# A fused attention and mixture-of-experts kernel: its last group of tokens in eight plain products in place of seven with sums

## The chip, the cores and the metric

One Trainium2 chip, of which this kernel uses one core. A core has a matrix engine (TensorE, PE in the profile; its weight loads are PEld), a vector engine (VectorE, DVE), a scalar engine (ScalarE, ACT), a general engine (GpSimd, POOL) and a queue engine for transfers (SyncE, SP). Each works through its own instructions in order; they meet at semaphores. Matmul results land in PSUM, which has eight banks of 128 x 512 fp32 numbers; POOL does not read it in this kernel. The metric is the device time of one execution in microseconds (us); lower is better.

## The reference

Linear attention with exponential features on 8 batches x 8 heads x 576 positions gives x of 4608 x 512. A routing table P of 4608 x 8 comes from x by alternate normalising, and eight experts are added up, every token through every expert:

```python
out = np.zeros((N, D), dtype=np.float32)      # N = 4608, D = 512
for e in range(E):                            # E = 8
    h = np.maximum(x @ w1[e], 0.0)            # w1[e]: 512 x 1024
    ye = h @ w2[e]                            # w2[e]: 1024 x 512
    out += P[:, e:e + 1] * ye
```

## The kernel before

**Tiling.** The tokens are in nine groups of 512: groups 0 to 7 are the first 512 positions of each batch, group 8 is what is left of all batches. The attention comes first, with expert 0 between its pieces; then the experts 1 to 7, one after the other. `acc[g]` holds a group's 512 x 512 fp32 result in SBUF (four blocks `ts` of 128 tokens), and each expert adds to it. The last expert (e = 7) takes group 8 first, then the pairs of groups 0-1, 2-3, 4-5, 6-7, and stores each group's result when it is done.

**Two products per expert and group.** The up-projection (`up7`) makes h in bf16, in tiles `hT` of 128 x 2 x 512: `H[j][k]` of a group is half j of the 1024 hidden features, in two tiles. The down-projection (`down7`) makes h @ w2. Both use a scheme of seven products for a 2 x 2 split in place of eight (Strassen's, in Winograd's form): some operands are sums of quarters. In `down7` the halves are i (256 tokens each), j (hidden features, then output columns). The sums of w2's quarters (`T` tiles) are made once per expert; the last expert leaves w2 itself whole. The sums of h, S0 to S3, are made per group by DVE: eight instructions of 128 x 512 (`sub`, whose `f.tensor_tensor` is L1013), into `S` tiles, and for the very last group into `hT` tiles.

**The seven products** of a group are named X1, X2, X3, X4, Y1, Z1, Z2. Each is eight matmuls of 256 columns (`product`, L1130: two blocks of 128 tokens, four steps over 512 hidden features). They use three PSUM banks, x, y and z. Those of one letter add up in one bank: X1 is done and read out, then X2 is added on top and read out, and so on. Where they go, as (token half, column half) of `acc[g]`: X1 and Y1 to (0,0), X2 and Z2 to (0,1), Z1 and X3 to (1,1), X4 to (1,0). X1 multiplies w2 and h themselves, Y1 also; X2, Z1, X3 and Z2 have a sum of h on the left; X2, Z1, X3, X4 a sum of w2 on the right.

**Reading a product out** (`read`) has two ways. Either DVE does it in two instructions of 128 x 256, bank times P plus `acc` (L1306). Or ACT scales the bank into a tile (two instructions, L1316; tile `V`, in the end `U`) and POOL adds it to `acc` (one of 128 x 512, L1320). ACT's scalings carry a common key, "order of V", so that they run in the order in which they were emitted.

**The order of work** is the program's own. `Plan` collects operations in the order in which the code emits them, with an engine, a duration, a latency and what they depend on, and `Plan.schedule` writes out one order for every engine: at each step it takes the operation that can start earliest, and among those the one emitted first. The chip's engines then follow that order, with semaphores for the true dependencies. The plan holds a few dependencies that are there for order alone: X1 lists the keys of S1 and S2, Z1 that of S3, and POOL's adds at the end those of "sums of h".

**The main loop** interleaves by `ORDER` the up-projection of one pair with the down-projections of the pair before, taken from `queue`. When the last pair, groups 6 and 7 of expert 7, is up, nothing is left to interleave with: `d6` and `d7` are the two down-projections left over, and the list `END` says in which order their products are emitted ("a" for group 6, "b" for group 7). `store` issues the results from SP, for these two groups by quarters as soon as both products of a quarter are in: 256 KB each, and the quarter (1,0) of group 6 in two of 128 KB.

Of the kernel before, what the change touches and what calls it, by code (L numbers as in the profile page):

```python
# [228 lines left out]
def kernel(  # L229
# [1009 lines left out]
    def acc_part(g, i, j):  # L1239
        return lambda: acc[g][:, 2 * i:2 * i + 2, 256 * j:256 * j + 256]  # L1240

    def down7(e, g, H, B7, last=False):


        def part(i, j, h):
            return lambda: H[j][h]()[:, :, 256 * i:256 * i + 256]

        def hk(i, j, h=None):
            if h is None:
                return hk(i, j, 0) + hk(i, j, 1)  # L1250
            return [(H[j][h], i)] if g == 8 else [(H[j][h], n) for n in range(2)]

        def a(i, j):
            return lambda k, n: H[j][k // 2]()[:, k % 2, 256 * i + 128 * n:][:, 0:128]

        late = akey(g)
        S = [new("hT" if last else "S") for _ in range(4)]

        def sv(n):
            return S[n]().rearrange("p a b -> p (a b)").rearrange("p (a b) -> p a b", a=4)  # L1260

        def sh(n, h):
            return lambda: sv(n)[:, 2 * h:2 * h + 2, :]

        def s(n):
            return lambda k, i: sv(n)[:, k, 128 * i:128 * i + 128]

        def sk(n):
            return [(S[n], h) for h in range(2)]

        def s2():
            for h in range(2):
                sub(dve, 512, sh(2, h), part(0, 0, h), part(1, 0, h), ALU.subtract,
                    hk(0, 0, h) + hk(1, 0, h) + ["sums of h"], [(S[2], h)])

        if not last:
            s2()
        for h in range(2):
            sub(dve, 512, sh(0, h), part(1, 0, h), part(1, 1, h), ALU.add,
                hk(1, 0, h) + hk(1, 1, h) + ["sums of h"], [(S[0], h)])  # L1280
        for h in range(2):
            sub(dve, 512, sh(1, h), sh(0, h), part(0, 0, h), ALU.subtract,
                [(S[0], h)] + hk(0, 0, h), [(S[1], h)])
        if last:
            s2()
        for h in range(2):
            sub(dve, 512, sh(3, h), part(0, 1, h), sh(1, h), ALU.subtract,
                [(S[1], h)] + hk(0, 1, h), [(S[3], h)] + (["sums of h"] if h else []))

        def prod(bank, lhs, y, r, first, more=()):  # L1290
            f, r2 = B7[y]
            product(bank, lhs, lambda k: f()[:, k, :], 4,
                    r + r2 + (["P"] if e else late) + list(more), first)

        by_dve = ("X2", "Z2", "X4")
        ending = e == E - 1 and g in (6, 7)
        if ending:
            by_dve = by_dve + ("X3", "Y1", "Z1") if g == 6 else by_dve

        def read(bank, i, j, name):  # L1300

            if name not in by_dve:
                return read2(bank, i, j)
            for n in range(2):
                ts = 2 * i + n
                dve(330, lambda n=n, ts=ts: nc.vector.scalar_tensor_tensor(  # L1306
                    out=acc[g][:, ts, 256 * j:256 * j + 256],
                    in0=bank()[:, 256 * n:256 * n + 256], scalar=P[:, 4 * g + ts, e:e + 1],
                    in1=acc[g][:, ts, 256 * j:256 * j + 256], op0=ALU.mult, op1=ALU.add),
                    [bank, "P"], [("acc", g, ts, j)])  # L1310

        def read2(bank, i, j):

            u = new("U" if ending else "V")
            for n in range(2):
                act(390, lambda n=n: nc.scalar.activation(  # L1316
                    out=u()[:, n, :], in_=bank()[:, 256 * n:256 * n + 256], func=ACT.Copy,
                    bias=0.0, scale=P[:, 4 * g + 2 * i + n, e:e + 1]), [bank, "P"],
                    [(u, n), "order of V"])
            pool(670, lambda: nc.gpsimd.tensor_tensor(  # L1320
                out=acc[g][:, 2 * i:2 * i + 2, 256 * j:256 * j + 256],
                in0=acc[g][:, 2 * i:2 * i + 2, 256 * j:256 * j + 256], in1=u(), op=ALU.add),
                [(u, 0), (u, 1)] + ["sums of h"] * ending,
                [("acc", g, 2 * i + n, j) for n in range(2)])

        if e == 1 and g < 9:
            for ts in range(4):
                act(512, lambda ts=ts: nc.scalar.activation(
                    out=acc[g][:, ts, :], in_=acc[g][:, ts, :], func=ACT.Copy, bias=0.0,
                    scale=P[:, 4 * g + ts, 0:1]), ["P", ("acc", g, ts)] + akey(g)  # L1330
                    + ([("acc", g - 2, 0, 0)] if g >= 2 else []),
                    [("acc", g, ts, j) for j in range(2)])
        x, y, z = new("P1"), new("P1"), new("P1")

        def X1():
            prod(x, a(0, 0), "11", hk(0, 0), True, sk(1) + sk(2))
            read(x, 0, 0, "X1")

        def Y1():
            prod(y, a(0, 1), "21", hk(0, 1), True)  # L1340
            read(y, 0, 0, "Y1")

        def Z1():
            prod(z, s(0), "t1", sk(0), True, sk(3))
            read(z, 1, 1, "Z1")

        def X2():
            prod(x, s(1), "t2", sk(1), False)
            read(x, 0, 1, "X2")

        def X3():
            prod(x, s(2), "t3", sk(2), False)
            read(x, 1, 1, "X3")

        def Z2():
            prod(z, s(3), "22", sk(3), False)
            read(z, 0, 1, "Z2")

        def X4():
            prod(x, a(1, 1), "t4", hk(1, 1), False)  # L1360
            read(x, 1, 0, "X4")

        def stores(names):
            if e < E - 1:
                return
            if g not in (6, 7):
                for ts in range(4 if len(names) == len(all_) else 0):
                    store(g, ts)
                return
            for i, j, by in ((0, 0, {"X1", "Y1"}), (0, 1, {"X2", "Z2"}), (1, 1, {"Z1", "X3"}),  # L1370
                             (1, 0, {"X4"})):
                if by <= names and (i, j) not in stored:
                    stored.add((i, j))
                    one = (g, i, j) == (6, 1, 0)
                    for n in range(2 if one else 1):
                        store(g, 2 * i + n, (j,), 1 if one else 2)

        all_ = {"X1": X1, "Y1": Y1, "Z1": Z1, "X2": X2, "X3": X3, "Z2": Z2, "X4": X4}
        emitted, stored = set(), set()

        def step(name):
            all_[name]()
            emitted.add(name)
            stores(emitted)

        return step


    ORDER = "X1 x10 w10 x11 X2 x20 y10 x21 Z1 y11 X3 w11 x30 x31 x40 x41 w20 Y1 w21 X4 Z2".split()
    END = (  # L1390
        "aX1 bY1 aX2 bX1 bX2 bZ1 aZ1 aX3 aY1 aZ2 bX3 bX4 bZ2 aX4").split()
    queue = []

    def pop():
        if not queue:
            return None
        e, g, H, B7 = queue.pop(0)
        return down7(e, g, H, B7, (e, g) == (E - 1, 7))

    for e in range(1, E):  # L1400
        w1, w2 = load_w(e, ["late"] + [("acc", 8, ts, j) for ts in range(4) for j in range(2)
                                       if e > 1])
        if e == 1:
            for p in range(4):
                pair_sums_x(p)
            sums_x(8)
            for p in range(4):
                seen = {}
                for key in xkeys(2 * p):
                    for d in plan.readers.get(key, []):  # L1410
                        seen[id(d)] = d
                grant("X", p, seen.values())
        A7, B7 = sums_w(e, w1, w2)
        for p in (range(5) if e < E - 1 else (4, 0, 1, 2, 3)):
            X = load_x(p)
            gs = (2 * p, 2 * p + 1) if p < 4 else (8,)
            H = [[[new("hT") for _ in range(2)] for _ in range(2)] for _ in gs]
            un = up7(A7, p, X, H, ["up0"])
            for half in range(len(gs)):
                dn = pop()  # L1420
                for n in ORDER:
                    if len(n) == 3:
                        un[n[:2], int(n[2]) + 2 * half]()
                    elif dn is not None:
                        dn(n)
            queue += [(e, g, h, B7) for g, h in zip(gs, H)]
    d6, d7 = pop(), pop()
    for n in END:
        (d6 if n[0] == "a" else d7)(n[1:])
    plan.run(tc)  # L1430


# [28 lines left out]
```

## Time and profile before

| | |
|---|---|
| time, median of 3 runs | 1035.03 us (1034.81 to 1035.73) |
| the profiled execution: its time | 1034.76 us |
| the profiled execution: its span, first to last instruction | 1032.9 us |
| mean granted clock of TensorE | 0.997 |
| bytes moved by transfers | 93.77 MB |
| seven products of groups 6 and 7, from the first matmul to the start of the last | 1010.92 to 1027.64 us |

In the lines of the profile a matmul or other instruction stands as line, engine, operation, what it writes "<-" what it reads, and "xN" for how many of a kind in a row. In the timeline the first two numbers are the start and the length in us, and a bracket at the end gives idle time of the engine ahead of it and who ended it. Matmuls overlap, so that one lasts 0.27 us though the next follows after 0.11. In the names of a product, `w` is a quarter of w2, `T` a sum of its quarters, `hT` a quarter of h (or, for the last group, a sum in a borrowed tile) and `S` a sum of h.

### The profile page before, as it was taken

How to read it: one execution, taken by the hardware profiler on the slowest of the kernel's cores; microseconds unless marked ns; L12 is line 12 of the kernel's file. 1: busy time of each engine (PE TensorE's matmuls, PEld its weight loads, DVE VectorE, ACT ScalarE, POOL GpSimd, SP SyncE). 2: the span in 40 equal slices, each digit the busy share in tenths (PEclk: the TensorE clock that was granted, in tenths of full speed). 3: DMA queues.
4: the chain of work that ended last, by engine and by line, in shares of the span. 5: the costliest groups of instructions: out<-in, count | busy, mean ns of one | idle time of the engine just before them, and what ended most of it. 6: DMA issues, size and time to landing. Idle time of an engine off the chain costs nothing.

```text
span 1032.9 us, 21788 instructions
## 1 busy us (share of the span) xinstructions
PE 1007.7 (98%) x7856; PEld 692.4 (67%) x7974; DVE 874.4 (85%) x1875; ACT 707.5 (68%) x1571; POOL 466.8 (45%) x535
## 2 busy tenths in 40 slices
PE   7899999999999999999999999999999999999997
PEld 5666666644566766676667666676667666776665
DVE  7999998987787888888878888888888888887887
ACT  7999999845688766566666665666666665656662
POOL 5877775400244444434444354435343444344443
PEclk9999999999999999999999999999999999999998
DMA  9998985095311152122511161106111421104323
GB/s 259 179 171 143 183 156 103 2 230 145 75 43 51 52 107 58 42 63 51 114 42 54 40 128 48 41 22 123 48 47 52 99 65 42 62 22 123 133 92 123
DMA packets 124700, 93.77 MB, mean 91 GB/s; under 512 B 47456, under 2 KB 116640, under 8 KB 124592
## 3 DMA queue, kind: packets, MB, share of 16 engines
q1 hardware_dynamic: 90832, 68.44, 24.3%
q0 software_dynamic: 33680, 23.90, 16.2%
q8 instruction: 62, 1.02, 0.4%
q14 instruction: 46, 0.38, 0.1%
q10 hardware_dynamic: 80, 0.03, 0.0%
HBM read 94.98 MB, written 14.16 MB: 106 GB/s over the span
## 4 chain that ended last, share of the span: by engine, by line
PE 90%; DVE 6%; DMA 1%; issue 1%; ACT 1%; SPq 0%; POOL 0%; DVEq 0%; ACTq 0%
PE P L1130 40%; PE P L1164 30%; PE P L484 17%; DVE acc L1306 1%; PE P L683 1%; DMA acc<-in_q_dram 1%; DVE hT L1194 1%; DVE m L476 1%; DVE w L1013 1%; PE P L722 1%; DVE hT L1013 1%; DVE S L1013 0%; SPq L406 0%; PE P L688 0%; DVE xb L703 0%
## 5 line engine op out<-in xcount | busy, mean ns | idle before, releaser
L1320 POOL TENSOR_TENSOR acc<-acc,V 128x512 f32<-128x512 f32 x244 | 313.9, 1298 | 433.4 <-ACT V L1316 430.0
L1190 ACT COPY U<-P 128x512 f32<-128x512 f32 x378 | 216.2, 588 | 133.4 <-PE P L1164 68.9
L1316 ACT ACTIVATE V<-P 128x256 f32<-128x256 f32 x488 | 212.8, 477 | 122.1 <-PE P L1130 118.6
L1194 DVE CUSTOM_DVE_ANT_0 hT<-P,U 128x512 bf16<-128x512 f32 x378 | 252.3, 687 | 36.6 <-ACT U L1190 21.0
L1130 PEld LDWEIGHTS <-S 128*128 128x128 bf16 x1984 | 194.5, 98 | 56.0 <-issue 3.0
L1306 DVE SCALAR_TENSOR_TENSOR acc<-P,acc 128x256 f32<-128x256 f32 x384 | 164.7, 478 | 72.4 <-PE P L1130 69.9
L1164 PE MATMUL P<-xT,w 128*128 128x512 bf16 x682 | 193.3, 379 | 1.8 <-DVE acc L1306 0.6
L1130 PEld LDWEIGHTS <-hT 128*128 128x128 bf16 x1544 | 151.4, 98 | 56.4 <-DVE hT L1194 0.7
L1164 PE MATMUL P<-xT,T 128*128 128x512 bf16 x544 | 156.8, 379 | 1.6
L1130 PE MATMUL P<-w,hT 128*128 128x256 bf16 x1016 | 146.7, 273 | 0.4 <-DVE hT L1194 0.3
L1130 PE MATMUL P<-T,S 128*128 128x256 bf16 x1056 | 137.7, 273 | 2.8 <-DVE acc L1306 2.6
L1164 PEld LDWEIGHTS <-w 128*128 128x128 bf16 x896 | 87.6, 98 | 61.2 <-issue 0.7
L1130 PE MATMUL P<-w,S 128*128 128x256 bf16 x928 | 124.1, 273 | 1.1
L1013 DVE TENSOR_TENSOR S<-hT 128x512 bf16<-128x512 bf16 x248 | 105.1, 439 | 19.3 <-PE P L1130 18.3
L1164 PEld LDWEIGHTS <-T 128*128 128x128 bf16 x672 | 65.7, 98 | 58.0 <-issue 1.8
L476 DVE TENSOR_REDUCE m<-P 128x4 f32<-128x512 f32 x128 | 83.7, 679 | 3.4 <-PE P L484 2.4
L609 POOL TENSOR_TENSOR v<-v_m,em 128x512 bf16<-128x512 f32 x64 | 66.9, 1045 | 43.2 <-ACT em L480 39.1
L1199 ACT ACTIVATE hT<-P 128x512 bf16<-128x512 f32 x126 | 74.2, 598 | 11.7 <-PE P L1164 11.4
L484 PE MATMUL P<-xT,w 128*128 128x512 bf16 x271 | 71.7, 379 | 0.9 <-ACT q L480 0.3
L1130 PE MATMUL P<-T,hT 128*128 128x256 bf16 x528 | 71.3, 275 | 0.0
L484 PE MATMUL P<-w,hT 128*128 128x512 bf16 x272 | 69.7, 379 | 0.8 <-DVE m L476 0.2
L480 ACT ACTIVATE k<-P 128x512 bf16<-128x512 f32 x128 | 68.8, 633 | 2.2 <-PE P L484 1.3
(109 smaller groups left out, 1178.5 us busy)
## 6 DMA issues: line engine op xcount, KB each, us to landing
xT<-xd SPq DMA_DIRECT2D x168, 128.0 KB, 2.2
w<-in_moe_w_dram POOLq DMA_DIRECT2D x14, 1024.0 KB, 9.9
v_m<-in_v_dram SPq DMA_DIRECT2D x14, 512.0 KB, 5.1
out_dram<-acc SPq DMA_DIRECT2D x12, 512.0 KB, 3.1
X<-xd SPq DMA_DIRECT2D x42, 128.0 KB, 2.2
early<-xd SPq DMA_DIRECT2D x42, 128.0 KB, 2.2
xd<-S SPq DMA_DIRECT2D x18, 256.0 KB, 2.9
qk<-in_k_dram POOLq DMA_DIRECT2D x12, 256.0 KB, 5.5
```

The lines of the kernel that those rows point to most:

```text
L476: dve(el, lambda: nc.vector.tensor_reduce(out=dst(), in_=src(), axis=AX.X, op=ALU.max, apply_absolute_value=True), r, w)
L480: act(el, lambda: nc.scalar.activation(out=dst(), in_=src(), func=ACT.Exp, bias=0.0, scale=scale), r, w)
L484: nc.tensor.matmul(out_, lhsT=lhsT, rhs=rhs, start=start, stop=stop)
L1013: lambda: f.tensor_tensor(out=out_(), in0=x(), in1=y(), op=op), r, w, **kw)
L1130: pe(256, lambda i=i, k=k, z=z: nc.tensor.matmul(bank()[:, 256 * i:256 * i + 256], lhsT=lhs(k, i), rhs=rhs(k), start=first and z, stop=k = ...
L1164: pe(512, lambda k=k: nc.tensor.matmul(bank[fp](), lhsT=f()[:, k, 128 * fp:128 * fp + 128], rhs=rhs(k), start=first and k == 0, stop=k == ...
L1190: act(512, lambda: nc.scalar.copy(out=u[fp][n]().rearrange("p a b -> p (a b)"), in_=x[fp]()), [x[fp]], [u[fp][n]])
L1194: dve(500, lambda: nc.vector._custom_dve(ADD_SAT, out=out_(fp, i, j), in0=halves_(bank[fp]()), in1=flat(u[fp][n]()), s0=3.0e38, s1=0.0), [ ...
L1199: act(512, lambda: nc.scalar.activation(out=out_(fp, i, j), in_=halves_(x[fp]()), func=ACT.Relu, bias=0.0, scale=1.0), [x[fp]], [okey(fp, ...
L1306: dve(330, lambda n=n, ts=ts: nc.vector.scalar_tensor_tensor(out=acc[g][:, ts, 256 * j:256 * j + 256], in0=bank()[:, 256 * n:256 * n + 256 ...
L1316: act(390, lambda n=n: nc.scalar.activation(out=u()[:, n, :], in_=bank()[:, 256 * n:256 * n + 256], func=ACT.Copy, bias=0.0, scale=P[:, 4 ...
L1320: pool(670, lambda: nc.gpsimd.tensor_tensor(out=acc[g][:, 2 * i:2 * i + 2, 256 * j:256 * j + 256], in0=acc[g][:, 2 * i:2 * i + 2, 256 * j: ...
```

## The change

Group 7 of the last expert is no longer done by `down7`. A new function `down8` makes its down-projection as plain products: for each block of 128 tokens, all 512 columns and all 1024 hidden features in eight matmuls of 512 columns into a bank of its own, then one DVE instruction that adds bank times P to `acc`, then one store of 256 KB. The order of the blocks is 2, 3, 0, 1, and block 1 is done in two halves of 256 columns, each in a bank of its own, with its own read and its own store of 128 KB. Group 7 needs no sums of h and no `hT` tiles for them. `END` lets these blocks take turns with the seven products of group 6, whose order changes. Group 6 now reads X2, Z2 and X4 by DVE and X1, Y1, Z1 and X3 by ACT and POOL (before: X1 alone that way, and group 7's X1, Y1, Z1 and X3); POOL's adds no longer list "sums of h"; and its quarter (1,0) is stored in one piece.

```diff
-    def down7(e, g, H, B7, last=False):
+    def down7(e, g, H, B7):
...
-        S = [new("hT" if last else "S") for _ in range(4)]
+        S = [new("S") for _ in range(4)]
...
-        if not last:
-            s2()
+        s2()
...
-        if last:
-            s2()
...
-        ending = e == E - 1 and g in (6, 7)
+        ending = e == E - 1 and g == 6
         if ending:
-            by_dve = by_dve + ("X3", "Y1", "Z1") if g == 6 else by_dve
+            by_dve = ("X2", "Z2", "X4")
...
-                [(u, 0), (u, 1)] + ["sums of h"] * ending,
+                [(u, 0), (u, 1)],
                 [("acc", g, 2 * i + n, j) for n in range(2)])
...
-            if g not in (6, 7):
+            if g != 6:
...
-                    one = (g, i, j) == (6, 1, 0)
-                    for n in range(2 if one else 1):
-                        store(g, 2 * i + n, (j,), 1 if one else 2)
+                    store(g, 2 * i, (j,), 2)
...
+    def down8(e, g, H, w2):
+
+        def chunk(ts, parts):
+            n = DD // parts
+            for c in range(parts):
+                py, cols = new("P1"), slice(n * c, n * c + n)
+                for fc in range(8):
+                    ht = H[fc // 4][fc % 4 // 2]
+                    pe(n, lambda py=py, ht=ht, fc=fc, cols=cols, n=n: mm(
+                        py()[:, 0:n], ht()[:, fc % 2, ts * 128:ts * 128 + 128],
+                        w2()[:, fc, cols], fc == 0, fc == 7),
+                        [(H[j][h], i) for j in range(2) for h in range(2) for i in range(2)]
+                        + [(w2, i, j) for i in range(2) for j in range(2)] + ["P"], [py])
+                js = range(2) if n == DD else (c,)
+                dve(580 * n // 512, lambda py=py, cols=cols, n=n:
+                    nc.vector.scalar_tensor_tensor(
+                        out=acc[g][:, ts, cols], in0=py()[:, 0:n],
+                        scalar=P[:, 4 * g + ts, e:e + 1], in1=acc[g][:, ts, cols],
+                        op0=ALU.mult, op1=ALU.add),
+                    [py, "P"], [("acc", g, ts, j) for j in js])
+                store(g, ts, js)
+
+        return chunk
+
...
-    END = (
-        "aX1 bY1 aX2 bX1 bX2 bZ1 aZ1 aX3 aY1 aZ2 bX3 bX4 bZ2 aX4").split()
+    END = "aX1 aY1 b2 aX2 aZ1 b3 aX3 aX4 b0 aZ2 b1".split()
...
-        e, g, H, B7 = queue.pop(0)
-        return down7(e, g, H, B7, (e, g) == (E - 1, 7))
+        e, g, H, B7, w2 = queue.pop(0)
+        if (e, g) == (E - 1, 7):
+            return down8(e, g, H, w2)
+        return down7(e, g, H, B7)
...
     for n in END:
-        (d6 if n[0] == "a" else d7)(n[1:])
+        if n[0] == "a":
+            d6(n[1:])
+        else:
+            d7(int(n[1]), 2 if n == "b1" else 1)
```

More of the change, by code (lines that the diff above doesn't have):

```diff
@@ L1425 @@
                         dn(n)
-            queue += [(e, g, h, B7) for g, h in zip(gs, H)]
+            queue += [(e, g, h, B7, w2) for g, h in zip(gs, H)]
     d6, d7 = pop(), pop()
     for n in END:
-        (d6 if n[0] == "a" else d7)(n[1:])
+        if n[0] == "a":
+            d6(n[1:])
+        else:
+            d7(int(n[1]), 2 if n == "b1" else 1)
     plan.run(tc)
```

## The prediction

> **What bounds the kernel now.** I read the page first: its engine table and its chain of waits, the one followed back from the last instruction.
>
> ```profile
> span 1032.9 us, 21788 instructions
> PE 1007.7 (98%) x7856; PEld 692.4 (67%) x7974; DVE 874.4 (85%) x1875; ACT 707.5 (68%) x1571; POOL 466.8 (45%) x535
> PE 90%; DVE 6%; DMA 1%; issue 1%; ACT 1%; SPq 0%; POOL 0%; DVEq 0%; ACTq 0%
> ```
>
> TensorE (PE) is the bound for the whole span; what the diff touches is only what follows the last up-projection, so I next read the chain in order of time from 1009 us on.
>
> ```profile
> 1010.25 1.75 DVE acc L1306 x4
> ...
> 1013.25 5.89 DVE hT L1013 x8
> 1019.14 0.80 DVE acc L1306 x2
> 1019.93 0.04 issue
> 1019.98 6.21 PE P L1130 x40
> 1026.18 0.02 issue
> 1026.21 2.23 DVE acc L1306 x5
> 1028.44 0.39 DVEq L1456
> ```
>
> In the last 23 us the chain leaves PE: for 5.89 us it runs through eight VectorE (DVE) instructions that write hT from hT. In this kernel only the sums of group 7 do that (they borrow hT buffers). The timeline by engine shows what they hold up.
>
> ```profile
> 1010.04 1.04 PE L1130 MATMUL P<-w,S 128*128 128x256 bf16 x8
> 1010.92 2.78 PE L1130 MATMUL P<-w,hT 128*128 128x256 bf16 x24
> 1013.54 2.12 PE L1130 MATMUL P<-T,S 128*128 128x256 bf16 x16
> 1015.50 1.04 PE L1130 MATMUL P<-w,hT 128*128 128x256 bf16 x8
> 1016.37 1.04 PE L1130 MATMUL P<-T,hT 128*128 128x256 bf16 x8
> 1019.98 1.10 PE L1130 MATMUL P<-T,S 128*128 128x256 bf16 x6 [2.57 <-DVE acc L1306]
> ...
> 1027.64 0.27 PE L1130 MATMUL P<-T,hT 128*128 128x256 bf16 x1
> ...
> 1014.65 5.61 POOL L1320 TENSOR_TENSOR acc<-acc,U 128x512 f32<-128x512 f32 x4 [3.47 <-ACT U L1316]
> 1019.06 2.43 DVE L1306 SCALAR_TENSOR_TENSOR acc<-P,acc 128x256 f32<-128x256 f32 x6
> ```
>
> The row at 1010.04 is group 5's last product (Z2). From 1010.92 on, PE runs the fourteen products of groups 6 and 7: 24 matmuls for Y1 of both and X1 of group 6, 16 for Z1 and X2 of group 6, 8 + 8 for X1 and Z1 of group 7. Then it stands still for 2.57 us: X3 of group 6 adds into the bank of X2, so it needs X2's two DVE reads, and these start only at 1019.06, behind the eight sums. The sums are this late because five run at about 0.42 us and three, beside POOL's adds, at up to 1.49 us:
>
> ```profile
> L1013 DVE TENSOR_TENSOR hT<-hT x8: 418/420/1492, 1013.2 to 1017.7; 128x512 bf16<-128x512 bf16 x8
> ```
>
> The gap has a second price. The table by stretches gives the granted clock (the value ahead of the last two):
>
> ```profile
> 1010.90:1017.30 6.40, 6.35 (x58) 5.48 (x57) 6.33 (x13) 2.30 (x6) 2.93 (x3) 1.00 0.43 166
> 1017.40:1019.90 2.50, 0.01 (x1) 0.00 (x0) 2.50 (x5) 0.85 (x3) 2.40 (x3) 1.00 0.00 0
> 1020.40:1023.70 3.30, 3.30 (x18) 2.34 (x17) 1.97 (x6) 0.00 (x0) 0.00 (x0) 0.50 0.36 126
> 1023.80:1027.70 3.90, 3.90 (x38) 3.42 (x35) 3.03 (x8) 0.84 (x2) 0.99 (x1) 1.00 0.44 153
> ```
>
> Just after the gap the clock is 0.50 for some 3.3 us. Pace at full clock: 24 matmuls in 2.78 us, the last lasting 0.27, so (2.78 - 0.27) / 23 = 0.109 us each. The 112 matmuls of both groups would take 12.21 us; from 1010.92 to the end of the last one's slot (1027.64 + 0.11) they take 16.83. Lost: 4.62, of which the gap (1017.24, where the next matmul was due, to 1019.98) is 2.74, a wait near 1014.5 some 0.2, and the half clock the rest, 1.68.
>
> **The change, part by part.**
>
> *The sums of group 7 go*: eight DVE instructions, 5.89 us of the chain. They are worth what they held up, 2.74 and 1.68, if PE always has other work.
>
> *Group 7's products*: seven of eight 256-column matmuls become three blocks of eight 512-column ones and one block in two halves, each eight of 256.
>
> ```profile
> 999.63 1.67 PE L1164 MATMUL P<-xT,w 128*128 128x512 bf16 x7
> L1164 PE MATMUL P<-xT,w 128*128 128x512 bf16 x682 | 193.3, 379 | 1.8 <-DVE acc L1306 0.6
> ```
>
> Seven of 512 columns in 1.67 us, the last lasting 0.379: 0.215 each. So 24 x 0.215 + 16 x 0.109 = 5.16 + 1.74 = 6.90 us in place of 56 x 0.109 = 6.10. Cost 0.80, all on PE, which sets the end.
>
> *The order.* The planner takes, at each step, the operation that can start earliest, and among equals the one emitted first. At 1010.92 X1 is not allowed yet (the plan lets it wait for the sums S1 and S2 of group 6), Y1 is, and it comes before block 2. I carry that on by hand, with the plan's own latencies for what is ready, and these rows for how long work lasts; three sums of group 6 stand where they stood:
>
> ```profile
> 1011.91 0.41 DVE L1013 TENSOR_TENSOR S<-hT 128x512 bf16<-128x512 bf16 x1
> 1012.36 0.43 DVE L1013 TENSOR_TENSOR S<-S,hT 128x512 bf16<-128x512 bf16 x1
> 1012.82 0.43 DVE L1013 TENSOR_TENSOR S<-hT,S 128x512 bf16<-128x512 bf16 x1
> 1016.57 1.71 ACT L1316 ACTIVATE U<-P 128x256 f32<-128x256 f32 x4 [1.26 <-PE P L1130]
> L1306 DVE SCALAR_TENSOR_TENSOR acc<-P,acc 128x256 f32<-128x256 f32 x22 | 9.3, 476 | 2.3 <-PE P L1130 2.2
> ```
>
> PE: Y1 1010.92; block 2, seven matmuls, 1011.79; X1 1013.30; block 2's eighth 1014.17; Z1 1014.39; block 3, two, 1015.26; X2 1015.69; block 3, six, 1016.56; block 0, one, 1017.86; X3 1018.07; block 0, seven, 1018.94; X4 1020.45; Z2 1021.32; the halves of block 1 at 1022.19 and 1023.06; end of the slots 1023.92, of the last matmul 1024.08 (0.27 long in place of 0.109).
>
> *The waits that take the removed one's place* are the links of group 6's bank x. X1 ends at 1014.33 and ACT reads it twice, 0.84 us (half of the four in 1.71): done 1015.2, X2 is due at 1015.69. X2 ends 1016.72, DVE's two reads (0.40 and 0.48) are done at 1017.63, X3 is due at 1018.07. X3 ends 1019.1, ACT done 1020.0, X4 due 1020.45. Each has some 0.4 us to spare, and the cover is a block of group 7 every time; without it each link would cost about 1.1 us of PE.
>
> *Reads 512 wide on DVE* (three) are not in the trace. Below, one of 256 (0.476); above, two of them (0.95). Nearest is the row of the same width with PSUM and SBUF inputs:
>
> ```profile
> L1194 DVE CUSTOM_DVE_ANT_0 hT<-P,U 128x512 bf16<-128x512 f32 x378 | 252.3, 687 | 36.6 <-ACT U L1190 21.0
> ```
>
> I take 0.69. Block 2's read runs from 1014.65 to 1015.35, X2's need DVE at 1016.76; block 0's from 1020.65 to 1021.34, X4's at 1021.5. At 0.95 X4's reads slip by 0.1 and nothing at the end moves. Cost nothing.
>
> *Reads moved from DVE to ACT and POOL* (X3, Y1, Z1 of group 6, while group 7's own leave them): ACT takes them in the order of emission, POOL's four adds at 1.30 to 1.45 (5.61 in all before) run from 1015.25 to about 1021.4, each long before the end. The sums they slowed are gone; group 6's are over at 1013.25, before POOL begins. Nothing.
>
> *Stores*: nine in both versions on SP's one queue, but five belong to group 7 and start from 1015.4 on. The end decides:
>
> ```profile
> 1028.36 0.48 DVE L1306 SCALAR_TENSOR_TENSOR acc<-P,acc 128x256 f32<-128x256 f32 x1
> 1028.86 0.37 SPq L982 DMA_DIRECT2D out_dram<-acc  x1
> 1029.28 0.49 SPq L982 DMA_DIRECT2D out_dram<-acc  x1
> DMA to landing us min/median/max: 2.5/2.5/2.5
> ```
>
> Now the last matmul ends at 1027.91, two reads end at 1028.84, one store is issued and behind it the last at 1029.28: 1.37 us. It lands 2.5 later, and 1.1 us after that the span ends. After the change one 256-wide read follows the last matmul (0.04 + 0.48), then one 128 KB store at once (0.02), as the one ahead of it leaves SP by 1024.3 (its half is read by 1023.75, the issue takes up to 0.49): 0.54. Gain 0.83. The landing I leave at 2.5, as it is the same 128 KB.
>
> **Sum**: 1027.91 - 1024.08 = 3.83, and 0.83: 4.66 us. The profiled execution took 1034.76, 1.86 of it around the span: 1034.76 - 4.66 = 1030.1. It stood 0.27 below the median of the three runs shown (1035.03); against that it is 1030.4. I say 1030.2. Its own range is 1029.3 (landing in 2.2, no small waits left) to 1031.2 (the three links short by their 0.4 each).
>
> [...] The trace has the clock at 0.50 behind an idle time of 2.57 us, so the measurement decides for the gap.
>
> **Rivals.**
>
> 1. *The blocks go first.* If the planner spends group 7's work before X1 may start, bank x's links stand alone at the end. X1 would start at 1010.92 + 0.87 + 6.90 = 1018.69; three links of 0.87 + 0.16 + 0.04 + 0.84 + 0.05 = 1.96 bring X4 to 1024.6, its reads to 1026.5, the span to 1030.2, the time to 1032.0; with another half clock, 1033.7. For it: X1 did come third, after both Y1. Against it: it becomes ready at about 1013, when block 2 is not through.
>
> 2. *The half clock isn't the gap's doing* and comes back in the same place: then 1.68 is not won, 1031.8. For it: only one such stretch in the tail, one gap. Against it: the clock was 1.00 with PE busy from 1010.90 to 1017.30, and is so again at 1023.80. [...]
>
> 3. *The gap stays*: the sums weren't the cause, or the change lets another engine be late by as much. 1030.1 + 2.57 + 1.68 = 1034.4, no change that can be told. Against it: the chain runs through all eight sums without a break.
>
> 4. *Slower*: PE, which is in order, stands at X2 or X3 for s us because the read ahead of it is late, with all of both groups behind it, and the clock drops. The time is 1030.1 + s + 1.68, and exceeds 1035.03 by 0.2% from s = 5.3 us. For it: PE already waits 2.57 us at this link. Against it: ahead of X1's read on ACT stands no other read of the tail, ahead of X2's on DVE one of 0.69 us.
>
> **How the numbers follow.** Forecast 0.74, rival 1 0.10 (0.03 of it with the half clock), rival 2 0.05, rival 3 0.05, rival 4 0.06. About 0.2% (2.1 us) is what a measurement can tell from no change here. Faster: forecast, rival 2 and most of rival 1, 0.86. Same: rival 3 and the rest of rival 1, 0.08. Slower 0.06. The range, 1029.3 to 1032.2, takes in the forecast's own, rival 2 and rival 1 without the clock.
>
> **What would show it.** No DVE instruction writes hT from hT; PE has no idle over 0.3 us from 1010.9 on and a granted clock of 1.00 to the end; its last matmul ends near 1024.1; the 512-wide reads last 0.6 to 0.75; the last store is issued some 0.55 us behind the last matmul; the span is near 1028.2. A gap on PE ahead of a T,S product, or a stretch at 0.50, would prove the order wrong; a last store that waits for another on SP, the end.

## The result, and the profile after

The changed kernel takes 1030.32 us (median of 6 runs, 1029.93 to 1030.77), the kernel before 1034.92 (6 runs, 1033.29 to 1035.73): a ratio of 0.9957 with a 95% interval of 0.9945 to 0.997. That is 4.6 us faster; the forecast was a time of 1030.2 us. The profiled execution took 1030.37 us.

The page of the kernel after, in the same lines as before:

```profile
span 1028.6 us, 21737 instructions
PE 1006.3 (98%) x7838; PEld 690.2 (67%) x7958; DVE 866.7 (84%) x1860; ACT 706.6 (69%) x1569; POOL 465.1 (45%) x534
PE 91%; DVE 4%; DMA 1%; issue 1%; ACT 1%; SPq 0%; POOL 0%; DVEq 0%; ACTq 0%
```

DVE's share of the chain fell from 6% to 4%. The chain in order of time shows what it lost (start, length, what; all in us):

```profile
1009.75 2.62 PE P L1130 x24
1012.37 0.05 issue
1012.43 1.46 PE P L484 x6
...
1022.79 1.76 PE P L484 x16
1024.56 0.02 issue
1024.58 0.48 DVE acc L1399
```

The chain now stays on PE from the last up-projection to the last matmul; one read of 0.48 us ends it. PE's timeline (L484 is the helper that issues the blocks' matmuls) gives the order:

```profile
1010.46 1.04 PE L1130 MATMUL P<-w,S 128*128 128x256 bf16 x8
1011.34 1.04 PE L1130 MATMUL P<-w,hT 128*128 128x256 bf16 x8
1012.43 1.46 PE L484 MATMUL P<-w,hT 128*128 128x512 bf16 x6
1013.72 1.04 PE L1130 MATMUL P<-w,hT 128*128 128x256 bf16 x8
1014.60 0.38 PE L484 MATMUL P<-w,hT 128*128 128x512 bf16 x1
1014.81 1.04 PE L1130 MATMUL P<-T,S 128*128 128x256 bf16 x8
1015.68 0.59 PE L484 MATMUL P<-w,hT 128*128 128x512 bf16 x2
1016.12 1.04 PE L1130 MATMUL P<-T,S 128*128 128x256 bf16 x8
1016.99 1.67 PE L484 MATMUL P<-w,hT 128*128 128x512 bf16 x7
1018.50 1.04 PE L1130 MATMUL P<-T,S 128*128 128x256 bf16 x8
1019.37 1.67 PE L484 MATMUL P<-w,hT 128*128 128x512 bf16 x6
1020.88 1.04 PE L1130 MATMUL P<-T,hT 128*128 128x256 bf16 x8
1021.76 1.04 PE L1130 MATMUL P<-w,S 128*128 128x256 bf16 x8
1022.63 1.91 PE L484 MATMUL P<-w,hT 128*128 128x256 bf16 x16
```

The first row is group 5's last product (Z2), as before. Behind it stand Y1, block 2, X1, the rest of block 2, Z1, two matmuls of block 3, X2, the rest of it with one of block 0, X3, block 0, X4, Z2, block 1. No row has a bracket: the profile shows no wait of PE. (Two of the 24 matmuls of 512 columns left no record, so that two rows count six for seven.) One stretch holds it all, with the granted clock at 1.00 (the value ahead of the last two):

```profile
1011.30:1024.50 13.20, 13.10 (x96) 9.31 (x96) 7.65 (x16) 3.14 (x8) 5.32 (x5) 1.00 0.50 185
```

Executions differ before this part even begins: it begins 1011.11 us after the start in the profile of e6 below and 1012.83 us after it in that of e7, and these two kernels differ only in what comes later. So I also compare the **tail**: from the start of the first matmul behind group 5's Z2 (1010.92 before, 1011.34 after) to the end of the span. It fell from 21.98 to 17.22 us, by 4.76; the prediction's sum was 4.66.

### The profile page after: what moved, and what is told of

Same layout as the page of the kernel before. It is cut to its first block, busy times and chain, and to the rows that moved or that the text cites. A ratio compares the mean times of both kernels' runs of the same rounds, so it can differ in the third digit from the quotient of the medians.

```text
span 1028.6 us, 21737 instructions
## 1 busy us (share of the span) xinstructions
PE 1006.3 (98%) x7838; PEld 690.2 (67%) x7958; DVE 866.7 (84%) x1860; ACT 706.6 (69%) x1569; POOL 465.1 (45%) x534
## 4 chain that ended last, share of the span: by engine, by line
PE 91%; DVE 4%; DMA 1%; issue 1%; ACT 1%; SPq 0%; POOL 0%; DVEq 0%; ACTq 0%
PE P L1130 40%; PE P L1164 31%; PE P L484 18%; PE P L683 1%; DVE acc L1303 1%; DVE hT L1194 1%; DMA acc<-in_q_dram 1%; DVE w L1013 1%; PE P L722 1%; DMA acc<-in_k_dram 1%; DVE m L476 0%; SPq L406 0%; PE P L688 0%; DVE S L1013 0%; ACT k L480 0%
## 5 line engine op out<-in xcount | busy, mean ns | idle before, releaser
L1303 DVE SCALAR_TENSOR_TENSOR acc<-P,acc 128x256 f32<-128x256 f32 x372 | 159.6, 477 | 71.7 <-PE P L1130 69.2
L1130 PEld LDWEIGHTS <-hT 128*128 128x128 bf16 x1488 | 145.5, 98 | 55.8 <-DVE hT L1194 0.7
L1130 PE MATMUL P<-w,hT 128*128 128x256 bf16 x992 | 143.7, 273 | 0.4 <-DVE hT L1194 0.3
L484 PE MATMUL P<-w,hT 128*128 128x512 bf16 (+1 forms) x310 | 77.3, 373 | 0.9 <-DVE m L476 0.2
L484 PE MATMUL P<-xT,w 128*128 128x512 bf16 x271 | 71.7, 379 | 0.9 <-ACT q L480 0.3
L480 ACT ACTIVATE q<-P 128x512 bf16<-128x512 f32 x128 | 69.4, 639 | 0.4
```

The costliest lines, as they stand in the source:

```text
L480: act(el, lambda: nc.scalar.activation(out=dst(), in_=src(), func=ACT.Exp, bias=0.0, scale=scale), r, w)
L484: nc.tensor.matmul(out_, lhsT=lhsT, rhs=rhs, start=start, stop=stop)
L1130: pe(256, lambda i=i, k=k, z=z: nc.tensor.matmul(bank()[:, 256 * i:256 * i + 256], lhsT=lhs(k, i), rhs=rhs(k), start=first and z, stop=k = ...
L1303: dve(330, lambda n=n, ts=ts: nc.vector.scalar_tensor_tensor(out=acc[g][:, ts, 256 * j:256 * j + 256], in0=bank()[:, 256 * n:256 * n + 256 ...
```

## The experiments

Every kernel below computes the whole result; where work is added, nothing reads it. The tail and its two parts come from the profile of one execution each, the time is the median of all runs with its count.

| kernel | time (us) | ratio to before, 95% interval | tail | last matmul ends after | from there to the last store's issue |
|---|---|---|---|---|---|
| before | 1034.92 (6) | | 21.98 | 17.00 | 1.37 |
| after | 1030.32 (6) | 0.9957, 0.9945 to 0.997 | 17.22 | 13.20 | 0.55 |
| e1: before, GpSimd held | 1030.83 (4) | 0.9956, 0.9941 to 0.9971 | 17.88 | 12.61 | 1.37 |
| e2: after, dead sums | 1030.68 (4) | 0.9956, 0.994 to 0.9973 | 17.42 | 13.20 | 0.76 |
| e3: after, blocks first | 1032.1 (5) | 0.9968, 0.9955 to 0.9982 | 19.05 | 14.33 | 0.94 |
| e4: after, block 1 whole | 1031.01 (4) | 0.9959, 0.9944 to 0.9974 | 17.60 | 13.18 | 0.82 |
| e5: after, three dead sums | 1033.6 (10) | 0.9992, 0.9981 to 1.0002 | 19.64 | 15.61 | 0.55 |
| e6: after, seven dead reads | 1033.21 (10) | 0.9985, 0.9974 to 0.9995 | 19.80 | 15.79 | 0.55 |
| e7: after, four dead reads | 1031.91 (10) | 0.997, 0.996 to 0.9979 | 18.64 | 14.62 | 0.55 |
| e8: e1, last stores split | 1031.22 (5) | 0.9964, 0.9951 to 0.9977 | 17.83 | 12.60 | 1.61 |
| e9: after, reads on DVE | 1030.87 (8) | 0.996, 0.9949 to 0.9971 | 17.53 | 13.20 | 0.88 |
| e10: after, twelve dead reads | 1036.76 (10) | 1.0019, 1.0007 to 1.003 | 23.10 | 19.09 | 0.55 |

**e1: the kernel before, with GpSimd held back.** Was it the eight sums that cost, or only that GpSimd ran beside three of them?

```diff
+        if last:
+            pool(1, lambda: nc.gpsimd.tensor_copy(out=held, in_=sv(3)[:, 3, 0:4]),
+                 sk(3), ["held"])
...
-                [(u, 0), (u, 1)] + ["sums of h"] * ending,
+                [(u, 0), (u, 1)] + ["sums of h", "held"] * ending,
```

> The kernel before, with one thing added: GpSimd copies four numbers of the last sum of group 7 before it starts the tail's adds, so that no add runs beside the sums. My theory: the 2.57 us gap on TensorE came from three sums that took 1.48 us beside GpSimd's adds in place of 0.42. Then all eight sums take 0.42 us or less, X2 of group 6 is read by about 5.9 us behind the tail's first matmul, no gap over 0.4 us is left on TensorE, the granted clock stays at 1.00, and from the tail's first matmul to the end of the span it takes 17.5 us (before: 21.95, after the change: 17.2); the time is about 1030.6. Rival: eight more instructions in DVE's queue are enough, whoever runs beside them. Then a gap of over 1 us stays and the time is over 1032.5.

The row of the sums before, and behind it the timelines of e1, DVE, GpSimd and PE:

```profile
1013.16 5.98 DVE L1013 TENSOR_TENSOR hT<-hT 128x512 bf16<-128x512 bf16 x8
```

```profile
1013.36 2.76 DVE L1014 TENSOR_TENSOR hT<-hT 128x512 bf16<-128x512 bf16 x8
1016.05 2.47 DVE L1311 SCALAR_TENSOR_TENSOR acc<-P,acc 128x256 f32<-128x256 f32 x6
...
1016.19 0.19 POOL L1292 COPY held<-hT 128x4 bf16<-128x4 bf16 x1 [4.81 <-DVE hT L1014]
1016.34 4.95 POOL L1325 TENSOR_TENSOR acc<-acc,U 128x512 f32<-128x512 f32 x4
...
1017.45 0.82 PE L1131 MATMUL P<-T,S 128*128 128x256 bf16 x6
```

The same eight sums last 2.76 us in place of 5.98, X2 is read from 1016.05 on, and X3 follows at 1017.45 without a wait. GpSimd's first add starts 5.2 us behind the tail's first matmul in place of 3.7; holding it back for these 1.5 us gives 4.1 of the 4.76 us, with seven products for group 7 and all its sums. My theory holds; the gap was made by three sums beside GpSimd's adds, not by sums as such.

**e2: the changed kernel, with group 7's sums left in.** Its edit is `down7`'s four sums, two halves each, put into `down8` with four `hT` tiles of their own:

```diff
     def down8(e, g, H, w2):
 
+        S = [new("hT") for _ in range(4)]
...
+        for h in range(2):
+            sub(dve, 512, sh(0, h), part(1, 0, h), part(1, 1, h), ALU.add,
+                hk(1, 0, h) + hk(1, 1, h) + ["sums of h"], [(S[0], h)])
...
```

> The changed kernel with the eight sums of group 7 left in as dead work (nothing reads them). My theory: the sums are what cost, in whatever order the products stand. GpSimd's adds start about 4.4 us behind the tail's first matmul and stretch the last sums to 1.4 us each; X2 of group 6 is read some 3 us late, TensorE stands for 2 us or more before X3, the clock drops to 0.50 behind it, and the tail takes 20 to 21.5 us; the time is 1033 to 1034.7. Rival: the new order is what helps, the blocks of group 7 fill any wait. Then the tail stays at 17.2 to 17.6 and the time at 1030.3 to 1030.7.

My expectation failed. DVE in e2, the last of its eight sums, and GpSimd's first add:

```profile
1013.53 2.77 DVE L1013 TENSOR_TENSOR hT<-hT 128x512 bf16<-128x512 bf16 x8
...
1015.88 0.42 DVE L1013 TENSOR_TENSOR hT<-hT 128x512 bf16<-128x512 bf16 x1
...
1015.66 1.77 POOL L1317 TENSOR_TENSOR acc<-acc,U 128x512 f32<-128x512 f32 x1 [4.11 <-ACT U L1313]
```

I had counted a sum at 0.42 us, its length; from start to start it is 2.77 less 0.42, over 7, 0.34. So six are done when GpSimd begins, and the seventh is under way. The eighth starts beside the add and by my theory should have taken some 1.4 us, but it took 0.42, and the add took 1.77 us in place of the 1.27 that the next two took: here GpSimd was held up and not DVE. Why the turn fell that way is not shown. GpSimd begins 4.4 us behind the tail's first matmul, against 3.7 in the kernel before (1014.65 less 1010.92), since block 2 now stands ahead of X1, whose read sets GpSimd off. The sums of group 7 cost the new order 0.2 us of tail. This run doesn't say what several sums would cost beside GpSimd in the new order; e5 does.

**e5: three dead sums, placed beside GpSimd's adds.**

```diff
             prod(x, s(1), "t2", sk(1), False)
+            if ending:
+                dum = new("hT")
+                dve(1, lambda: [nc.vector.tensor_tensor(
+                    out=dum().rearrange("p a b -> p (a b)").rearrange(
+                        "p (a b) -> p a b", a=4)[:, 2 * (k % 2):2 * (k % 2) + 2, :],
+                    in0=part(0, 0, 0)(), in1=part(1, 0, 0)(), op=ALU.subtract)
+                    for k in range(3)],
+                    [x] + hk(0, 0, 0) + hk(1, 0, 0), [dum])
             read(x, 0, 1, "X2")
```

> The changed kernel with three dead sums (bf16, 512 wide, both inputs in SBUF) put on DVE just ahead of X2's reads, unknown to the plan, at a time when GpSimd runs three adds in a row. My theory: beside GpSimd each takes some 1.4 us from one start to the next, as before the change; they last 4.2 us in place of 1.0, X2's reads start 2.8 us late, TensorE stands some 2.5 us ahead of X3, and the tail grows from 17.2 to about 19.7 us, or 21.4 if the clock drops too. Rival (GpSimd is not the cause of the long sums): 1.0 us in all, over before X2 is done; the tail stays at 17.2 to 17.4.

```profile
1015.16 4.32 DVE L1348 TENSOR_TENSOR hT<-hT 128x512 bf16<-128x512 bf16 x3
...
1015.13 4.07 POOL L1317 TENSOR_TENSOR acc<-acc,U 128x512 f32<-128x512 f32 x3 [4.11 <-ACT U L1313]
...
1020.32 1.03 PE L1130 MATMUL P<-T,S 128*128 128x256 bf16 x8 [2.24 <-DVE acc L1303]
```

Three sums take 4.32 us, about one of GpSimd's adds (4.07 / 3) each, and the gap ahead of X3 is back at 2.24 us. So the stretching works in the new order too, and the blocks of group 7 cover only some 0.4 us of lateness. The clock stayed at 1.00.

**e6, e7 and e10: a gap of a chosen length.** In place of e5's sums, dead reads of the bank (one input in PSUM, one in SBUF), seven, four or twelve. Of the two figures of e10 the one without is for a clock that stays at 1.00, the one with is for the half clock behind the gap, at the 1.7 us that it cost in the profile of before:

```diff
+                dum = new("V")
+                dve(1, lambda: [nc.vector.scalar_tensor_tensor(
+                    out=dum()[:, k % 2, :], in0=x()[:, 0:256], scalar=P[:, 4 * g, e:e + 1],
+                    in1=acc[g][:, 0, 256:512], op0=ALU.mult, op1=ALU.add)
+                    for k in range(7)],
+                    [x, "P"], [dum])
```

> The changed kernel with seven dead reads (bank times P plus acc, 256 wide) put on DVE ahead of X2's reads, unknown to the plan. They cost 0.40 us each, GpSimd or not, so that X2's reads start 2.8 us late and TensorE stands 2.4 us ahead of X3, much as it did before the change (2.57). My theory: a gap of that length brings the clock to 0.50 for 3.4 us behind it, which costs 1.7 more: the tail is 17.2 + 2.4 + 1.7 = 21.3 us, and the time 4 us longer than the changed kernel's. [...]

> The same with four dead reads: TensorE stands 1.2 us ahead of X3. My theory: a gap half as long leaves the clock at 1.00, and the tail is 17.2 + 1.2 = 18.4 us. Rival: any gap of over a microsecond brings the half clock; then it is 20.1.

> The changed kernel with twelve dead reads ahead of X2's: TensorE stands some 4.4 us. [...] Without it the tail is 17.2 + 4.4 = 21.6 us and the time 1034.8, with it 23.3 and 1036.5; I expect most times near the second. [...]

DVE, GpSimd and PE in e6, then its stretches ahead of the gap, behind it and later:

```profile
1017.06 2.83 DVE L1348 SCALAR_TENSOR_TENSOR V<-P,acc 128x256 f32<-128x256 f32 x7 [1.46 <-PE P L1130]
...
1015.49 3.84 POOL L1317 TENSOR_TENSOR acc<-acc,U 128x512 f32<-128x512 f32 x3 [4.11 <-ACT U L1313]
...
1020.86 1.03 PE L1130 MATMUL P<-T,S 128*128 128x256 bf16 x8 [2.43 <-DVE acc L1303]
```

```profile
1016.30:1019.60 3.30, 2.13 (x13) 1.09 (x12) 2.54 (x7) 0.57 (x2) 2.94 (x3) 1.00 0.38 142
1019.70:1023.00 3.30, 2.14 (x14) 1.36 (x14) 1.73 (x4) 0.84 (x2) 0.09 (x1) 1.00 0.23 88
1023.10:1026.40 3.30, 3.30 (x31) 2.86 (x30) 2.83 (x6) 0.00 (x0) 1.08 (x1) 1.00 0.39 135
```

Seven reads, all but the last begun beside GpSimd's adds, cost 0.40 each, as forecast, and make nearly the gap of before (2.43 against 2.57), but the clock stays at 1.00: the tail is 19.80 and not 21.3. For this profile my theory was wrong. The ten times of e6 run from 1032.3 to 1035.2; by the changed kernel's 1030.3 and the gap 1032.7 was due without the half clock and 1034.4 with it, so other executions may have paid it. The tail of e7 is 18.64 with a gap of 1.25 and the clock at 1.00, near the 18.4 of the theory. In e10 (gap 4.38) the clock fell:

```profile
1018.20:1021.50 3.30, 0.00 (x0) 0.00 (x0) 3.26 (x9) 0.00 (x0) 0.49 (x1) 1.00 0.23 79
1021.60:1024.90 3.30, 2.49 (x10) 1.57 (x11) 1.19 (x3) 0.81 (x2) 0.00 (x0) 0.50 0.21 79
```

Its median of 1036.76 lies by the figure with the half clock (1036.5), not by the one without (1034.8).

**e11 and e12: the kernel before, profiled again.** In one execution the clock's changes lie whole multiples of 3.41 us apart (before: 1020.37, 1023.78, 1030.61). I call a stretch of 3.41 us counted out from such a change a window, and its ends edges.

> The kernel before, unchanged, for a second profile. My theory: its 2.6 us gap costs the half clock only where it falls inside one window. The times of before so far lie in two groups (1032.5 to 1034.1 and 1034.6 to 1036.7), some 2 us apart. If the window's edge cuts the gap here, the clock stays at 1.00 behind it and the tail is 20.3 us in place of 21.98; if not, it is 22.0 again. Rival: the clock falls behind every such gap in this kernel; the tail is 22.0 in every execution.

> The same, for a third profile: the tail is 20.3 us where the edge of a window cuts the gap, and 22.0 where it doesn't; with the edges told by the clock's changes at the start of the execution, every 3.41 us. Rival as in the second profile.

The times were 1035.14 and 1035.19 us. Both tails were as long as the first, 21.99 and 22.02 us, and the clock fell to 0.50 in both, as the rival said. In the third an edge cut the gap, into 0.13 and 0.63 of a window, and the clock fell even so: my theory fails here, as an edge in the gap did not spare it. The share of each window touched that the gap takes up, and the clock in the window behind:

| execution | gap (us) | share of the windows touched | clock behind |
|---|---|---|---|
| before, first and second | 2.57 | 0.75 | 0.50 |
| before, third | 2.58 | 0.13, then 0.63 | 0.50 |
| e6 | 2.43 | 0.35, then 0.36 | 1.00 |
| e5 | 2.24 | 0.29, then 0.37 | 1.00 |
| e7 | 1.25 | 0.37 | 1.00 |
| e10 | 4.38 | 0.10, 1.00, 0.19 | 0.50 behind the second |

The third profile of before, in the two windows in question:

```profile
1018.30:1021.60 3.30, 1.22 (x12) 1.09 (x12) 3.30 (x7) 0.38 (x2) 2.37 (x2) 1.00 0.00 0
1021.70:1025.00 3.30, 3.30 (x18) 2.30 (x16) 2.34 (x7) 0.00 (x0) 0.00 (x0) 0.50 0.46 161
```

In these seven profiles the clock fell behind each window with a share of 0.63 or more and behind none with 0.37 or less. Two windows near the start of the program, each with the one behind it, the first pair of the changed kernel and the second of e6, show PE idle for shares between these:

```profile
8.28:11.69 3.41, 1.57 (x13) 1.20 (x12) 1.94 (x4) 3.41 (x10) 1.93 (x3) 1.00 0.94 235
11.70:15.11 3.41, 2.78 (x12) 1.72 (x12) 3.31 (x6) 2.98 (x9) 0.41 (x2) 0.50 0.98 315
```

```profile
9.29:12.70 3.41, 1.71 (x14) 1.28 (x14) 1.74 (x4) 3.15 (x9) 2.34 (x4) 1.00 1.00 280
12.80:16.00 3.20, 2.80 (x21) 1.92 (x20) 3.20 (x6) 3.20 (x12) 0.90 (x3) 1.00 0.95 299
```

With PE idle for 0.54 of a window the clock fell, with 0.50 it didn't. Counted out in this way, the first profile of before and that of the changed kernel have 601 whole windows: the clock fell behind three of them, idle for 0.54 (the pair above), 0.75 (the gap) and 0.79 (the end of before, from 1027.20 to 1030.61), and behind none of the others, idle for 0.41 or less.

I had expected from the times that before falls into two groups 2 us apart; with all its runs they are spread from 1032.5 to 1036.7 without a clear cut (one is at 1038.3). The mean clock of a run says more. A whole window at half clock takes 0.5 x 3.41 / 1033, or 0.0017, off it, so that a run with a mean of 0.999 can't have paid one in the tail. Of the 51 runs of before that were timed beside the experiments 18 had 0.999; their median is 1033.56 us, against 1035.29 for the other 33. Some of these can owe their lower clock to a fall at the start of the program, so how often before pays the half clock in the tail stays open; it is in 33 of the 51 at most.

**e3: all blocks first** (`END = "b2 b3 b0 b1 aX1 aY1 aX2 aZ1 aX3 aX4 aZ2"`).

> The changed kernel with another order of emission: all blocks of group 7 first, then group 6's products (rival 1 of the prediction). My theory: bank x's links stand alone at the end, TensorE waits some 0.8 us before X3 and little before X4, two reads and one 256 KB store follow the last matmul, and the tail takes 18.75 us in place of 17.2; the time is 1031.9. Rival: taking turns is worth nothing, since TensorE does the same work: the tail stays within 0.5 us of 17.2.

```profile
1011.49 7.09 PE L484 MATMUL P<-w,hT 128*128 128x512 bf16 x40
...
1022.82 1.03 PE L1130 MATMUL P<-T,S 128*128 128x256 bf16 x8 [0.75 <-DVE acc L1303]
```

The links of bank x stand alone and PE waits 0.75 us ahead of X3; the tail is 1.8 us longer than with turns, the time 1032.1. Of that, 1.1 us passes before the last matmul ends and 0.4 before the last store is issued, as here two reads follow the last matmul. Taking turns, with a half block at the end, is worth that much.

**e4: block 1 in one piece** (`d7(int(n[1]), 1)`).

> The changed kernel with the last block in one piece (eight matmuls of 512 columns, one read of 512, one store of 256 KB) in place of two halves. My theory: TensorE ends at the same place, the last read takes 0.75 us in place of 0.48 and the last store lands up to 0.2 us later: the tail takes 17.5 to 17.7 us, the time is 0.3 to 0.5 us longer than the changed kernel's. Rival: one read and one store fewer save more than the shorter last piece does: the tail is 17.2 or less.

The last read takes 0.75 us in place of 0.48, PE ends where it did, and the tail is 0.4 us longer, 17.60. Halving the last block is worth that.

**e8: e1 with the last store in two pieces** (`one = (g, i, j) == (7, 1, 0)` in place of `(6, 1, 0)`).

> The kernel before with GpSimd held until the sums are done (the first experiment), and besides group 7's quarter (1,0), the last to be read, stored in two pieces of 128 KB, group 6's in one. My theory: TensorE needs 0.6 us less than with eight products, and now only one 128 KB store follows the last read, so that the tail falls from 17.9 us to about 17.1, level with the changed kernel's 17.2. Rival: the order of the last stores is worth nothing, and the tail stays at 17.8 to 18.

The rival was right. SP's queue at the end of e8:

```profile
1024.21 2.04 SPq L983 DMA_DIRECT2D out_dram<-acc  x4
```

Four stores become due within a microsecond and SP issues one each 0.5 us, so the last waits for the three ahead of it: 1.61 us behind the last matmul. In the changed kernel the last two stores are issued 0.87 us apart, with the eight matmuls of a half block between what they wait for.

**e9: group 6's reads as before** (`by_dve = ("X2", "Z2", "X4", "X3", "Y1", "Z1")`).

> The changed kernel with group 6's reads as before the change: X1 alone by ACT and GpSimd, X3, Y1 and Z1 by DVE. My theory: the move of three reads off DVE was worth nothing by itself; DVE has the room, X3 stands a little later in the order, and the tail is 17.2 to 17.6 us, the time within 0.4 us of the changed kernel's. Rival: DVE becomes the bound of the tail with them, TensorE stands over 0.5 us at a link, and the tail is over 18.

PE ends at the same 13.20; the reads at the end queue a little on DVE and the tail is 17.53. The move to ACT and GpSimd was worth 0.3 us at most.

## Why the prediction was right

- **The bound and the gap.** The gap of 2.74 us from one matmul's slot to the next and the half clock behind it are gone, as read. That GpSimd's adds made three sums long was read off the trace; e1 and e5 show it. What the prediction gave too much weight is that the sums had to go: with GpSimd held for 1.5 us they may stay (e1), and in the new order all eight kept their short length (e2).
- **The price of the clock, 1.68 us**, is right for the profiled execution and for two more of the same kernel, but it is no fixed price of a gap of 2.57 us: e6 has nearly that gap and doesn't pay. Where the gap of before cost the term it filled 0.75 or 0.63 of a window, and in e6, with no more than 0.36 of one, it didn't; the prediction did not consider this. The forecast took the term in full, and that the medians bear it out is in part luck: at least 18 of 51 runs of before didn't pay the term, and their median is 1.7 us lower than that of the others.
- **The eighth product**, forecast at 0.80 us of PE: PE ends at 13.20 against 12.61 in e1, which has the short wait near Z1 (0.2 us) that the changed order lost. Right.
- **The order of PE** came out matmul for matmul. Its length was forecast at 13.16 us and is 13.20.
- **The links.** X1's two ACT reads end at 1015.64 and X2 follows at 1016.12; X2's reads end at 1018.14, X3 starts at 1018.50; X3's end at 1020.41, X4 starts at 1020.88. Spare 0.36 to 0.48, forecast 0.4. e5 and e6 show what happens beyond it: the lateness less 0.4 to 0.5 becomes a gap (X2's reads end 2.71 and 2.90 us later behind the tail's first matmul than in the changed kernel, the gaps are 2.24 and 2.43). e3 gives 1032.1 for the rival with the blocks first, forecast at 1032.0.
- **The read 512 wide** takes 0.751 us, between the bounds, above the 0.69 taken. It is on no path but the end of e4.
- **The end.** From the last matmul to the last store's issue 0.55 us, forecast 0.54; the landing took 2.3 and not 2.5.

```profile
L1399 DVE SCALAR_TENSOR_TENSOR acc<-P,acc 128x512 f32<-128x512 f32 x3 | 2.3, 751 | 3.7 <-PE P L484 3.7
1024.27 0.27 PE L484 MATMUL P<-w,hT 128*128 128x256 bf16 x1
1024.58 0.48 DVE L1399 SCALAR_TENSOR_TENSOR acc<-P,acc 128x256 f32<-128x256 f32 x1 [0.39 <-PE P L484]
DMA to landing us min/median/max: 2.3/2.3/2.3
```

- **The span** is 1028.6 where near 1028.2 was forecast. The tail began 0.42 us later than in the profile of before (1011.34 against 1010.92), ahead of anything the change touches.

## What to carry to other kernels

Ask of a late instruction on an engine not only how many stand ahead of it, but which of them is slow and beside what it runs: here one tiny copy that kept GpSimd off three vector sums was worth nearly as much as a new scheme for a whole group (4.1 us of tail against 4.76). In a tail in which each product waits for the read of the one before, put independent work between the links, and measure how much lateness it covers (0.4 us here). At the very end, count the chain behind the last matmul: width of the last read, stores due at once on one queue, the landing.

## What the runs showed of the hardware

- **Sums beside GpSimd's adds.** A DVE sum of two bf16 inputs in SBUF, 512 wide, took 0.42 us with no add beside it (e1: 2.76 us for eight) and up to 1.49 beside GpSimd's fp32 adds (before); in e5 three sums took 4.32 us beside three adds that took 4.07. It wasn't the sum that waited each time: in e2 one kept its 0.42 us and the add took 1.77 in place of 1.27. DVE reads with one input in PSUM and one in SBUF, six of seven begun beside the same adds, followed each other every 0.40 us, and the three adds took 3.84 (e6: 2.83 for seven reads; 3.83 for the adds in the changed kernel, which has no such reads). Why the sums grew long and the reads didn't, the runs don't show.
- **The clock.** The granted clock fell to 0.50 behind windows of 3.41 us in which PE had been idle for 0.54 of it (after), 0.63 (third profile of before), 0.75 (first) and 1.00 (e10), and stayed at 1.00 behind one idle for 0.50 (e6). In the tail of before it came back to 1.00 one window later (1020.37 to 1023.78). The gap of 2.57 us in before cost 1.68 us more in this way, that of 2.43 us in e6 nothing.
